# A recurrence and a routed mixture of experts on one core: layer two's matmuls after the last compaction, and five result buffers

## The chip, the core and the metric

The kernel runs on one core of a Trainium2 chip. A core has five engines that run side by side and meet only through semaphores: TensorE (PE) for matmuls and transposes, VectorE (DVE), ScalarE (ACT), GpSimd (POOL) and SyncE (SP). Matmuls write into PSUM, eight banks of 2 KB per partition; a bank holds 512 sums of 4 bytes for each of 128 partitions. DVE and ACT copy sums from PSUM to the on-chip memory SBUF; transfers between SBUF and the main memory are issued by SP, and, where rows are picked by an index, by POOL. The metric is the device time of one execution in microseconds (us); lower is better.

## The reference

```python
def _attn_ref(x, f_logit, lower_bound):            # x: 4 x 5056 x 256
    f = lower_bound + (1.0 - lower_bound) / (1.0 + np.exp(-f_logit))
    for t in range(S):
        h = f[:, t] * h + (1.0 - f[:, t]) * x[:, t]
        y[:, t] = h
...
def _moe_ref(x, w_gate, w1, w2):                   # N = 20224 rows, E = 8, F = 1024
    logits = x @ w_gate
    ...                                            # pairs by falling logit, at most N // E rows per expert
    for e in range(E):
        mask = assigned == e
        out[mask] = np.maximum(x[mask] @ w1[e], 0.0) @ w2[e]
```

A gated recurrence over 5056 time steps gives 20224 rows of 256 numbers. Every row is given to one of eight experts, 2528 rows to each, best logits first. An expert is two dense layers, 256 to 1024 with a relu and 1024 to 256.

## The kernel before

A first stage (to about 200 us) computes the recurrence with DVE scans, writes the rows to the buffer `hbuf` in main memory and collects the logits. The routing of the experts, one after the other, is a search on DVE with small matmuls. For each expert a *compaction* (`compact`, line 500) turns the mask of its rows into a list of row numbers; its matmuls write to the two PSUM banks `rt` and `rc` (lines 748 and 749). Routing and compaction of later experts run in small pieces (`tick`, line 1078) between the matmuls of the experts before them. The last compaction belongs to expert 7.

The rest is the experts' layers, in `moe` (line 755). An expert has 20 tiles of 128 rows, the last of 96, and they are worked in *chunks* of four tiles, five chunks per expert; expert 0 has six, and expert 7 six of 4, 4, 4, 4, 2 and 2 tiles. Layer one of a chunk is cut into eight blocks j of 128 hidden columns, and one block is a *step* of the loop at line 1098. A step holds, in PE's order:

- `first(k, c, j)`: six matmuls of 512 columns (the tiles' rows side by side) into a bank `pw`. There are six because every float32 number is split into a high and a low part (`xh`, `xl`, `w1h`, `w1l`) and three of the four products are kept, for each half of the 256 inputs. ACT then writes `hh`, the relu's high part, and DVE `hl`, its low part.
- in steps 3 and 5 (`TJ`), `trans`: the transposes `pt` of the next chunk's gathered rows `xg`, one half of the inputs in each.
- `second(...)`, layer two of the block three steps earlier (`LAG`): for each tile three matmuls of 256 columns, `hh` with the high part of w2, `hh` with its low part, `hl` with the high part, all added into the same 256 columns of a bank `py`, two tiles to a bank. So the last block of a chunk comes in step 2 of the next chunk; behind it ACT copies each bank to a result buffer `y` (pool `yp`, `YB` of them), which holds a pair of tiles.

POOL issues the transfers of this part: gathers of rows (`xg`, one per tile), stores of results (`out_dram`, one per tile), and three loads of weights per expert (`r`). They stand in one list, `issues`. `gather` appends a chunk's four (for the chunk after next, in step 0); `second` appends a chunk's stores; `load_w` puts its three at the list's front. At the end of each step one entry leaves the list (line 1125), and it waits on the chip for the newest `hh` that ACT had been given by then (`gate`). Three things take more than one out at once, and what stands ahead with it: `trans` forces the gathers that it is about to read (line 915), `split` the weights, and the claim of a result buffer all stores that are `YB` or more pairs old (line 977).

```python
            tc.add_manual_dep(st.ins, gate[-1].ins.name, SYNC, reason="one transfer per step")
...
            issue(upto=lambda what: what == ("g", k, c))
...
                issue(upto=lambda what: what[0] == "s" and what[1] <= turn - YB)
...
        issue(1 if i < len(todo) else 99, paced=i < len(todo))
```

The order on PE, DVE and ACT is the order in which this code emits instructions. A rough cost table (`Pace`) decides only when a waiting evacuation (`post`, `flush`) or a piece of the routing is emitted.

Of the kernel before, what the change touches and what calls it, by code (L numbers as in the profile page):

```python
# [7 lines left out]
F32 = mybir.dt.float32  # L8
# [5 lines left out]
AF = mybir.ActivationFunctionType  # L14
OP = mybir.AluOpType
# [91 lines left out]
def kernel(ctx: ExitStack, tc: tile.TileContext, x: bass.AP, f_logit: bass.AP,  # L107
# [643 lines left out]
    with tc.manual_schedule(engines={mybir.EngineType.PE, mybir.EngineType.DVE, mybir.EngineType.Activation}):  # L751
        moe(ctx, tc, locals())


def moe(ctx, tc, g):
    pace = g["pace"]
    nc = Paced(tc.nc, pace)
    v = nc.vector
    P, E, F, D, CAP, FB = (g[k] for k in ("P", "E", "F", "D", "CAP", "FB"))
    hbuf, w1, w2, out, ident_r, omlb, route, compact, rt, rc, ohp, ROW = (  # L760
        g[k] for k in ("hbuf", "w1", "w2", "out", "ident_r", "omlb", "route", "compact", "rt", "rc", "ohp", "ROW"))
# [3 lines left out]
    gp = ctx.enter_context(tc.tile_pool(name="gp", bufs=3))  # L765
    xp = ctx.enter_context(tc.tile_pool(name="xp", bufs=2))
    hp = ctx.enter_context(tc.tile_pool(name="hp", bufs=5))
    YB = 3
    yp = ctx.enter_context(tc.tile_pool(name="yp", bufs=YB))
    tps = ctx.enter_context(tc.tile_pool(name="tps", bufs=1, space=PSUM))  # L770
    pws = ctx.enter_context(tc.tile_pool(name="pws", bufs=3, space=PSUM))
    pys = ctx.enter_context(tc.tile_pool(name="pys", bufs=2, space=PSUM))
# [12 lines left out]
    WI, IDS, RAW, WS, XG, XS, HS, PY, SC = {}, {}, {}, {}, {}, {}, {}, {}, []  # L785
# [7 lines left out]
    issues = []  # L793
# [4 lines left out]
    def issue(n=1, upto=None, paced=False):  # L798
        st = None
        if upto is not None:  # L800
            n = max([x + 1 for x, (what, _) in enumerate(issues) if upto(what)], default=0)
        for _ in range(min(n, len(issues))):
            st = issues.pop(0)[1]()
            if paced and gate:

                tc.add_manual_dep(st.ins, gate[-1].ins.name, SYNC, reason="one transfer per step")
        return st
# [58 lines left out]
    def tiles(k, c):  # L866
        b, n = CHUNKS[k][c]
        return [min(P, CAP - (b + q) * P) for q in range(n)]

    def ids_at(k, c, q, n):  # L870
        b = CHUNKS[k][c][0] + q
        return off(IDS[k][:n, b:b + 1])
# [77 lines left out]
    def store(k, c, r, n, y):  # L950
        def emit():
            st = nc.gpsimd.indirect_dma_start(out=out, out_offset=ids_at(k, c, r, n), in_=y[:n, r % 2],
                                              in_offset=None)
            for o in SC:
                tc.declare_no_dep(st.ins, o.ins, reason="each row belongs to one expert")
            SC.append(st)
            return st
        return emit

    def second(k, c, j):  # L960
        hh, hl = HS.pop((k, c, j))
        w2s = WS[k][2]
        ns = tiles(k, c)
        for q, n in enumerate(ns):
            if j == 0 and q % 2 == 0:
                PY[q // 2] = pys.tile([P, 2, D], F32, name="py")
            if q:
                tick()
            py = PY[q // 2][:n, q % 2]
            a = slice(q * P, q * P + n)  # L970
            mm = [(hh[:, a], w2s[:, j, 0]), (hh[:, a], w2s[:, j, 1]), (hl[:, a], w2s[:, j, 0])]
            for i, (x, w) in enumerate(mm):
                nc.tensor.matmul(py, x, w, start=(j == 0 and i == 0 and q % 2 == 0),
                                 stop=(j == FB - 1 and i == 2), skip_group_check=True)
            if j == FB - 1 and q % 2 == 1:
                turn = len(SC) // 2 + sum(what[0] == "s" for what, _ in issues) // 2
                issue(upto=lambda what: what[0] == "s" and what[1] <= turn - YB)
                y = yp.tile([P, 2, D], F32, name="y")
                m = min(ns[q - 1:q + 1])
                if m == P:  # L980
                    nc.scalar.activation(y, PY[q // 2], AF.Copy)
                else:
                    nc.scalar.activation(y[:, 0], PY[q // 2][:, 0], AF.Copy)
                    nc.scalar.activation(y[:n, 1], py, AF.Copy)
                issues.extend((("s", turn), store(k, c, r, ns[r], y)) for r in (q - 1, q))

    class Bg:
        def __init__(self, gen, apart=0):
# [2 lines left out]
        def tick(self, force=False, within=None):  # L991
            if self.done:
                return False
            if within is not None:
                self.wait = min(self.wait, int(within))
            if not force:
                if self.wait:
                    self.wait -= 1
                    return False
                if not pace.due(self.need[0], self.need[1:], SLACK):  # L1000
                    return False
            try:
                self.need = next(self.gen)
                self.wait = self.apart
            except StopIteration:
                self.done = True
            return True
# [5 lines left out]
    comp, prog = {}, {}  # L1013
# [84 lines left out]
    for i in range(len(todo) + LAG):  # L1098
        step = i
        flush(i - 2 if i < len(todo) else i)  # L1100
        if i < len(todo):
            k, c, j = todo[i]
            if (c, j) == (0, 0) and k:
                assert wn == k + 1
                sp.until(lambda: sp.done)
                sp = None
            first(k, c, j)
            sp0.tick(True)
            tick()
            NS = len(CHUNKS[k])  # L1110
            if gathers:

                kk, cc = gathers[0]
                ahead = order.index((kk, cc)) - order.index((k, c))
                if ahead == 1 and j >= 1 or ahead == 2 and j >= (2 if (k, c) == (0, 0) else 0) and have(
                        kk, "ids", sum(CHUNKS[kk][cc])):
                    gather(*gathers.pop(0), soon=ahead == 1 or c == len(CHUNKS[k]) - 2 and j > 0)
            at = T0 if (k, c) == (0, 0) else TJ
            nxt = order.index((k, c)) + 1
            if j in at and nxt < len(order):  # L1120
                trans(*order[nxt], at.index(j))
        while made < first_lag.get(i, i - LAG + 1):
            second(*todo[made])
            made += 1
        issue(1 if i < len(todo) else 99, paced=i < len(todo))
        tick()
# [27 lines left out]
```

## Time and profile before

| | us |
|---|---|
| median of 3 runs | 1202.95 |
| the runs | 1202.89 to 1203.13 |
| the profiled execution, its own time | 1202.51 |
| its span | 1200.7 |
| PE busy | 1172.0 (98%) |
| DVE busy | 770.7 (64%) |
| ACT busy | 524.6 (44%) |
| POOL busy | 452.4 (38%) |

The span is what the profiler saw between the first and the last instruction; the execution's own time has 1.8 us around it. A share of busy time is a mean over stages with different limits, so the rows below are taken from stretches. In them a matmul's duration is longer than its distance from the next one, since matmuls are pipelined; what a matmul costs is read from the starts of a run of them.

### The profile page before, as it was taken

What the parts mean: (1) busy time and instruction counts of PE and PEld (TensorE: products, weight loads), DVE (VectorE), ACT (ScalarE), POOL (GpSimd) and SP (SyncE); (2) the same over time, 40 slices, a digit from 0 to 9 for tenths busy, and PEclk for the clock granted to TensorE, in tenths of its full rate; (3) what the DMA queues carried; (4) which work ended last, traced back from release to release, by engine and by line L of the source; (5) the groups of instructions that cost most, each with busy time, mean ns of one, the idle gap of its engine ahead of it and who ended that gap; (6) DMA issues with size and microseconds to landing.
All of it is one profiled execution on the core that took longest, in us unless ns stands there. A gap on an engine that the chain in (4) does not pass through costs nothing.

```text
span 1200.7 us, 23258 instructions
## 1 busy us (share of the span) xinstructions
PE 1172.0 (98%) x9152; PEld 1063.3 (89%) x9152; DVE 770.7 (64%) x1935; ACT 524.6 (44%) x1098; POOL 452.4 (38%) x458
## 2 busy tenths in 40 slices
PE   7999986999999999999999999999999999999997
PEld 7999965888988898888888888899889998999997
DVE  6999878878878977978788878423532243222222
ACT  7888813423533632632452345522642243223322
POOL 5777703332433324333333333333343334333322
PEclk9999998999999999999999999999999999999999
DMA  9999993112112212211211113111311131111111
GB/s 334 375 355 363 345 327 100 46 41 92 55 49 67 74 38 86 75 40 41 82 66 49 41 42 100 47 57 45 102 53 49 50 102 58 49 46 46 43 39 35
DMA packets 51869, 123.14 MB, mean 103 GB/s; under 512 B 7984, under 2 KB 28208, under 8 KB 50864
## 3 DMA queue, kind: packets, MB, share of 16 engines
q0 software_dynamic: 18960, 58.87, 15.7%
q1 hardware_dynamic: 32256, 62.78, 15.0%
q8 instruction: 72, 1.18, 0.4%
q14 instruction: 37, 0.30, 0.1%
q10 hardware_dynamic: 544, 0.01, 0.0%
HBM read 79.56 MB, written 42.07 MB: 101 GB/s over the span
## 4 chain that ended last, share of the span: by engine, by line
PE 61%; issue 19%; POOL 10%; DVE 4%; DMA 1%; POOLq 0%; ACT 0%; ACTq 0%; DVEq 0%; SPq 0%
PE py L100 25%; PE pw L100 24%; POOL out_dram L100 4%; POOL xg L100 4%; PE rt L100 4%; PE pr L100 4%; PE pb L100 2%; PE pf L100 2%; PE pt L100 1%; DVE MK L100 1%; POOL r L100 1%; DVE g L100 1%; DMA out_dram<-y,ids 0%; DMA fl<-in_f_logit_dram 0%; DMA xg<-hbuf,ids 0%
## 5 line engine op out<-in xcount | busy, mean ns | idle before, releaser
L100 PE MATMUL py<-w2s,hh 128*128 128x256 f32 (+1 forms) x2560 | 486.5, 287 | 0.6 <-ACT y L100 0.5
L100 ACT ACTIVATE hh<-pw 128x512 fp32r<-128x512 f32 (+3 forms) x336 | 192.5, 573 | 563.5 <-PE pw L100 541.2
L100 PEld LDWEIGHTS py<-w2s,hh 128*128 128x128 f32 (+1 forms) x2560 | 405.2, 187 | 19.2 <-ACT y L100 1.2
L100 DVE SCALAR_TENSOR_TENSOR hl<-pw,hh 128x512 fp32r<-128x512 f32 (+3 forms) x336 | 220.3, 656 | 313.7 <-ACT hh L100 312.6
L100 PE MATMUL py<-w2s,hl 128*128 128x256 f32 (+1 forms) x1280 | 361.3, 282 | 0.0
L100 POOL DMA_INDIRECT xg<-hbuf,ids x160 | 158.8, 992 | 313.9 <-ACT hh L100 292.6
L100 POOL DMA_INDIRECT out_dram<-y,ids x160 | 161.9, 1012 | 302.6 <-ACT hh L100 245.7
L100 PE MATMUL pw<-xh,w1h 128*128 128x512 f32 (+3 forms) x672 | 256.1, 383 | 2.4 <-DVE hl L100 1.7
L100 PE MATMUL pw<-xl,w1h 128*128 128x512 f32 (+3 forms) x672 | 257.7, 385 | 0.0
L100 PE MATMUL pw<-xh,w1l 128*128 128x512 f32 (+3 forms) x672 | 257.0, 384 | 0.0
L100 PEld LDWEIGHTS py<-w2s,hl 128*128 128x128 f32 (+1 forms) x1280 | 239.4, 187 | 0.0
L100 PEld LDWEIGHTS pw<-xh,w1l 128*128 128x128 f32 x672 | 125.9, 188 | 22.6
L100 PEld LDWEIGHTS pw<-xh,w1h 128*128 128x128 f32 x672 | 126.3, 189 | 14.4 <-DVE hl L100 1.9
L100 PEld LDWEIGHTS pw<-xl,w1h 128*128 128x128 f32 x672 | 126.0, 188 | 12.2 <-DVE r L100 0.2
L100 POOL TENSOR_TENSOR xl<-fl,xl 128x1024 f32<-128x1024 f32 (+1 forms) x39 | 92.3, 2366 | 42.8 <-ACT fl L100 35.1
L100 DVE TENSOR_TENSOR_SCAN g<-fg,g,pb 128x512 f32<-128x512 f32 (+4 forms) x78 | 92.8, 1227 | 9.9 <-ACT fg L100 8.9
L100 ACT ACTIVATE junk<-rt,r 128x158 bf16<-128x158 f32 x155 | 58.8, 392 | 53.9 <-DVE r L100 53.6
L100 PE MATMUL pr<-iw,g 128*128 128x136 f32 x632 | 79.8, 279 | 0.0
L100 PEld LDWEIGHTS pr<-iw,g 128*128 128x128 f32 x632 | 75.9, 190 | 0.1
L100 ACT ACTIVATE fg<-pf,one,nomlb 128x512 f32<-128x512 f32 (+1 forms) x80 | 57.4, 767 | 1.9
L100 ACT ACTIVATE y<-py 128x512 f32<-128x512 f32 (+2 forms) x88 | 48.1, 559 | 21.6 <-PE py L100 6.8
L100 DVE TENSOR_TENSOR xl<-pt,xh 128x512 fp32r<-128x512 f32 (+1 forms) x80 | 53.9, 674 | 0.6 <-ACT xh L100 0.3
(178 smaller groups left out, 1183.1 us busy)
## 6 DMA issues: line engine op xcount, KB each, us to landing
hbuf<-hr SPq DMA_DIRECT2D x39, 528.0 KB, 8.7
fl<-in_f_logit_dram SPq DMA_DIRECT2D x39, 512.0 KB, 5.9
xl<-in_x_dram SPq DMA_DIRECT2D x39, 512.0 KB, 6.1
xg<-hbuf,ids POOLq DMA_INDIRECT x160, 2.8
out_dram<-y,ids POOLq DMA_INDIRECT x160, 2.4
r<-in_moe_w_dram,wi POOLq DMA_INDIRECT x25, 4.5
hbuf<-hr SPq DMA_DIRECT2D x1, 264.0 KB, 9.1
fl<-in_f_logit_dram SPq DMA_DIRECT2D x1, 256.0 KB, 5.7
```

Of the source, the lines that this page charges most:

```text
L100: r = f(*args, **kw)
```

## The change

From the first chunk whose layer two begins after expert 7's compaction has ended, the two matmuls of a tile that share `hh` become one of 512 columns: the high and the low part of w2 lie side by side, and each gets its own 256 sums. A tile then fills a whole bank, the first two of a chunk in `py`, the third in `rt`, the fourth in `rc`. The matmul with `hl` adds to the first half. After a tile's last block ACT copies the second half to the result buffer, and DVE adds the first half to it. Apart from that, there are five result buffers in place of three, for the whole kernel.

```diff
-    YB = 3
+    YB = 5
...
+        if j == 0:
+            wides = len(ns) if E - 1 in comp and comp[E - 1].done else 0
+
+        def total(q):
+            y = Y[q // 2][:ns[q], q % 2]
+            v.tensor_tensor(y, PY[q][:ns[q], 0], y, op=OP.add)
+
+        def put(*qs):
+            issues.extend((("s", turn), store(k, c, r, ns[r], Y[r // 2])) for r in qs)
...
+                PY[q] = (pys.tile([P, 2, D], F32, name="py") if not wide or q < 2 else
+                         (rt, rc)[q - 2].tile([P, 512], F32, name="rt").rearrange("p (a d) -> p a d", a=2))
...
+            if wide:
+                nc.tensor.matmul(PY[q][:n], hh[:, a], w2s[:, j], start=(j == 0), stop=False, skip_group_check=True)
+                nc.tensor.matmul(PY[q][:n, 0], hl[:, a], w2s[:, j, 0], start=False, stop=last, skip_group_check=True)
...
+            if 0 < q <= wides:
+                total(q - 1)
+                if q % 2 == 0:
+                    put(q - 2, q - 1)
...
+            if wide:
+                nc.scalar.activation(Y[q // 2][:n, q % 2], PY[q][:n, 1], AF.Copy)
...
+            if wide and q == len(ns) - 1:
+                total(q)
+                put(q - 1, q)
```

Three places show what it does to the engines' orders. The first is PE in the first step with the merged form (third chunk of expert 5): `pt` are transposes, `py` and `rt` the banks of layer two.

```order
 L100 MATMUL pt<-identr,xg 128x128 x4
-L100 MATMUL py<-w2s,hh 128x256 x2
+L100 MATMUL py<-w2s,hh 128x512
 L100 MATMUL py<-w2s,hl 128x256
-L100 MATMUL py<-w2s,hh 128x256 x2
-L100 MATMUL py<-w2s,hl 128x256
-L100 MATMUL py<-w2s,hh 128x256 x2
-L100 MATMUL py<-w2s,hl 128x256
-L100 MATMUL py<-w2s,hh 128x256 x2
+L100 MATMUL py<-w2s,hh 128x512
 L100 MATMUL py<-w2s,hl 128x256
+L100 MATMUL rt<-w2s,hh 128x512
```

Each tile has two matmuls where it had three; the transposes keep their place ahead of layer two.

The second is ACT around the end of a late chunk, of before:

```order
L100 ACTIVATE xh<-pt 128x512
L100 ACTIVATE hh<-pw 128x512 x5
L100 ACTIVATE y<-py 128x512 x2
L100 ACTIVATE hh<-pw 128x512
L100 ACTIVATE xh<-pt 128x512
```

and now:

```order
L100 ACTIVATE xh<-pt 128x512
L100 ACTIVATE hh<-pw 128x512 x4
L100 ACTIVATE y<-py 128x256
L100 ACTIVATE hh<-pw 128x512
L100 ACTIVATE y<-py 128x256
L100 ACTIVATE y<-rt 128x256 x2
L100 ACTIVATE hh<-pw 128x512
```

The fifth `hh`, that of step 2, stood ahead of the copies and now stands behind the first of them. (On DVE the four additions stand between the `hl` of two steps.)

The third is POOL's list from the middle of expert 6's time on, before (`r` are weights, `xg` gathers, `out_dram` stores):

```order
L100 DMA xg<-hbuf,ids 128x264 x4
L100 DMA out_dram<-y,ids 20224x256 x2
L100 DMA r_12494<-in_moe_w_dram,wi 128x1024 x2
L100 DMA r_12495<-in_moe_w_dram,wi 128x2048
L100 DMA out_dram<-y,ids 20224x256 x2
L100 DMA xg<-hbuf,ids 128x264 x4
L100 DMA out_dram<-y,ids 20224x256 x5
L100 DMA xg<-hbuf,ids 128x264 x4
L100 DMA out_dram<-y,ids 20224x256 x5
```

and now, from a little earlier:

```order
L100 DMA xg<-hbuf,ids 128x264 x4
L100 DMA out_dram<-y,ids 20224x256 x4
L100 DMA xg<-hbuf,ids 128x264 x4
L100 DMA out_dram<-y,ids 20224x256 x4
L100 DMA xg<-hbuf,ids 128x264 x3
L100 DMA xg<-hbuf,ids 96x264
L100 DMA out_dram<-y,ids 20224x256 x4
L100 DMA xg<-hbuf,ids 128x264 x7
L100 DMA out_dram<-y,ids 20224x256 x4
L100 DMA xg<-hbuf,ids 128x264
L100 DMA r_12423<-in_moe_w_dram,wi 128x1024 x2
L100 DMA r_12424<-in_moe_w_dram,wi 128x2048
```

Stores no longer leave five in a row; they leave in fours, and seven gathers stand together once.

## Rows read from the trace of the kernel before

**Rows 1.** The profile's head and its line on PE: busy time, share of the span, instructions.

```profile
span 1200.7 us, 23258 instructions
PE 1172.0 (98%) x9152; PEld 1063.3 (89%) x9152; DVE 770.7 (64%) x1935; ACT 524.6 (44%) x1098; POOL 452.4 (38%) x458
```

**Rows 2.** Busy time by stretch, late in the layers: the stretch, its length, busy us of each engine with its instructions, then the granted clock, the DMA engines' share and GB/s.

```profile
800.00:900.00 100.00, 99.93 (x666) 90.53 (x665) 40.50 (x86) 44.63 (x102) 34.58 (x37) 1.00 0.20 64
900.00:1000.00 100.00, 99.79 (x656) 90.81 (x656) 35.90 (x53) 36.15 (x61) 35.57 (x37) 1.00 0.21 66
```

**Rows 3.** The chain that ended last, in order of time, in the middle of expert 7: start, length, what; `pw` are the six matmuls of a step's layer one (512 columns), `py` the twelve of its layer two (256 columns).

```profile
1095.07 1.40 PE pw L100 x6
1096.47 1.44 PE py L100 x12
...
1099.30 1.43 PE py L100 x12
1100.73 1.38 PE pw L100 x6
```

**Rows 4.** PE's instructions in order of time at the three places where ACT's copy waited for a store (start, length, what; in brackets the idle time ahead and what ended it), and the line of tile `y` on what ACT waited for (us, times).

```profile
626.67 0.27 PE L100 MATMUL py<-w2s,hl 128*128 128x256 f32 x1
627.22 0.38 PE L100 MATMUL py<-w2s,hh 128*128 128x256 f32 x1 [0.28 <-ACT y L100]
...
876.06 0.28 PE L100 MATMUL py<-w2s,hl 128*128 128x256 f32 x1
876.41 0.50 PE L100 MATMUL py<-w2s,hh 128*128 128x256 f32 x2
...
992.23 0.28 PE L100 MATMUL py<-w2s,hl 128*128 128x256 f32 x1
992.72 0.50 PE L100 MATMUL py<-w2s,hh 128*128 128x256 f32 x2 [0.21 <-ACT y L100]
...
  DMA out_dram<-y,ids: 6.2, 3
```

**Rows 5.** POOL's transfers in order of time: a chunk's end with stores in a burst, and the first and the fourth gather of a chunk four chunks later.

```profile
1014.74 0.97 POOL L100 DMA_INDIRECT out_dram<-y,ids  x1 [0.45 <-ACT y L100]
1016.01 0.97 POOL L100 DMA_INDIRECT out_dram<-y,ids  x1 [0.30 <-issue]
1017.28 0.97 POOL L100 DMA_INDIRECT out_dram<-y,ids  x1 [0.30 <-issue]
...
1105.85 0.99 POOL L100 DMA_INDIRECT xg<-hbuf,ids  x1 [1.92 <-ACT hh L100]
...
1114.68 0.94 POOL L100 DMA_INDIRECT xg<-hbuf,ids  x1 [1.89 <-ACT hh L100]
```

**Rows 6.** PE in order of time around steps 2 and 3 of that chunk: the last matmul of step 2's layer one, the last of the first tile's layer two, the transposes of step 3, and those of step 3 a chunk later.

```profile
1104.55 0.39 PE L100 MATMUL pw<-xh,w1l 128*128 128x512 f32 x1
...
1105.02 0.28 PE L100 MATMUL py<-w2s,hl 128*128 128x256 f32 x1
...
1107.61 0.46 PE L100 MATMUL pt<-identr,xg 128*128 128x128 f32 x4
...
1130.93 0.46 PE L100 MATMUL pt<-identr,xg 128*128 128x128 f32 x4
```

**Rows 7.** ACT at the same place: `hh` of step 2, `hh` of step 3 and the copy of the transposes behind it.

```profile
1104.98 0.60 ACT L100 ACTIVATE hh<-pw 128x512 fp32r<-128x512 f32 x1 [2.24 <-PE pw L100]
...
1107.81 0.60 ACT L100 ACTIVATE hh<-pw 128x512 fp32r<-128x512 f32 x1 [0.80 <-PE pw L100]
1108.31 0.59 ACT L100 ACTIVATE xh<-pt 128x512 fp32r<-128x512 f32 x1
```

**Rows 8.** A gather that PE waited for, early in the layers, in order of time; and of tile `xg` the time from a gather's start to its landing, and all that PE waited for it (us, times).

```profile
197.22 1.37 POOL L100 DMA_INDIRECT xg<-hbuf,ids  x1 [0.30 <-issue]
...
200.44 0.36 PE L100 MATMUL pt<-identr,xg 128*128 128x128 f32 x2 [0.93 <-DMA xg<-hbuf,ids]
...
  PE pt L100: 0.9, 1
...
DMA to landing us min/median/max: 2.7/2.8/3.8
```

**Rows 9.** Forms of ACT's and DVE's instructions behind 870 us: engine, operation, names, shapes, count, busy us, mean ns, idle time ahead.

```profile
L100 ACT ACTIVATE y<-py 128x256 f32<-128x256 f32 x3 | 1.1, 383 | 2.8 <-PE py L100 2.5
...
L100 DVE SCALAR_TENSOR_TENSOR hl<-pw,hh 128x256 fp32r<-128x256 f32 x8 | 3.4, 424 | 10.1 <-ACT hh L100 10.1
```

**Rows 10.** The end of the chain: start, length, what (a "q" is the engine's sequencer).

```profile
1191.71 2.87 PE py L100 x24
...
1194.61 0.38 ACT y L100
1194.99 0.28 ACTq L1150
1195.27 0.97 POOL out_dram L100
```

**Rows 11.** PE around 200 us by stretch (length, busy us, granted clock, DMA share, GB/s), and its longest idle time there, in order of time.

```profile
190.00:194.00 4.00, 1.10 (x7) 0.66 0.40 129
194.00:198.00 4.00, 4.00 (x33) 0.50 0.49 156
202.00:206.00 4.00, 2.31 (x17) 1.00 0.66 210
...
205.82 0.50 PE L100 MATMUL pw<-xh,w1h 128*128 128x256 f32 x2 [1.69 <-DVE hl L100]
```

More of the change, by code (lines that the diff above doesn't have):

```diff
@@ L958, in store @@
         return emit
+    Y, wides, turn = {}, 0, 0
     def second(k, c, j):
+        nonlocal wides, turn
         hh, hl = HS.pop((k, c, j))
@@ L963, in second @@
         ns = tiles(k, c)
+        last = j == FB - 1
+        if j == 0:
[5 more added lines that the diff above has]
+            issues.extend((("s", turn), store(k, c, r, ns[r], Y[r // 2])) for r in qs)
         for q, n in enumerate(ns):
-            if j == 0 and q % 2 == 0:
-                PY[q // 2] = pys.tile([P, 2, D], F32, name="py")
+            wide = q < wides
+            if j == 0 and (wide or q % 2 == 0):
+                PY[q] = (pys.tile([P, 2, D], F32, name="py") if not wide or q < 2 else
+                         (rt, rc)[q - 2].tile([P, 512], F32, name="rt").rearrange("p (a d) -> p a d", a=2))
@@ L967, in second @@
             if q:
                 tick()
-            py = PY[q // 2][:n, q % 2]
             a = slice(q * P, q * P + n)
[L971 to L975, printed above, removed]
+            if wide:
+                nc.tensor.matmul(PY[q][:n], hh[:, a], w2s[:, j], start=(j == 0), stop=False, skip_group_check=True)
+                nc.tensor.matmul(PY[q][:n, 0], hl[:, a], w2s[:, j, 0], start=False, stop=last, skip_group_check=True)
+            else:
+                py = PY[q - q % 2][:n, q % 2]
+                mm = [(hh[:, a], w2s[:, j, 0]), (hh[:, a], w2s[:, j, 1]), (hl[:, a], w2s[:, j, 0])]
+                for i, (x, w) in enumerate(mm):
+                    nc.tensor.matmul(py, x, w, start=(j == 0 and i == 0 and q % 2 == 0), stop=(last and i == 2),
+                                     skip_group_check=True)
@@ L976, in second @@
+            if not last:
+                continue
+            if 0 < q <= wides:
+                total(q - 1)
+                if q % 2 == 0:
+                    put(q - 2, q - 1)
+            if q % 2 == 0:
                 turn = len(SC) // 2 + sum(what[0] == "s" for what, _ in issues) // 2
                 issue(upto=lambda what: what[0] == "s" and what[1] <= turn - YB)
[L978 to L981, printed above, removed]
+                Y[q // 2] = yp.tile([P, 2, D], F32, name="y")
@@ L982, in second @@
+            if wide:
+                nc.scalar.activation(Y[q // 2][:n, q % 2], PY[q][:n, 1], AF.Copy)
+            elif q % 2 == 1:
+                y = Y[q // 2]
+                if n == P:
+                    nc.scalar.activation(y, PY[q - 1], AF.Copy)
                 else:
-                    nc.scalar.activation(y[:, 0], PY[q // 2][:, 0], AF.Copy)
+                    nc.scalar.activation(y[:, 0], PY[q - 1][:, 0], AF.Copy)
                     nc.scalar.activation(y[:n, 1], py, AF.Copy)
-                issues.extend((("s", turn), store(k, c, r, ns[r], y)) for r in (q - 1, q))
+                put(q - 1, q)
@@ L987, in moe @@
+            if wide and q == len(ns) - 1:
+                total(q)
+                put(q - 1, q)
     class Bg:
```

## The prediction

> **What bounds the kernel now.** I read the page first, for who is busy: the span is 1200.7 us and PE is busy in 98% of it [rows 1]. A busy PE is not yet a bound, so I took the table of stretches next: from 800 us on PE is busy in 99.8 to 99.9 of 100 us, while DVE, ACT and POOL stand at 35 to 45 [rows 2]. The chain of waits then says what a stretch of this part consists of: nothing but layer-one and layer-two matmuls in turn, a step of 6 and 12 of them [rows 3]. So here a nanosecond off a matmul is a nanosecond off the time, and so is every nanosecond for which PE has to wait; work on ACT, DVE and POOL costs nothing until it hands PE something late. The views to read next are therefore the few waits of PE that exist [rows 4], and how far ahead of PE the transfers run [rows 5 to 8].
>
> **Merged matmuls.** The program of after holds 416 matmuls of 512 columns in layer two, each in place of two of 256, from the third chunk of expert 5 on (13 chunks, 52 tiles, 8 blocks each). Twelve matmuls of 256 columns take 1.43 to 1.44 us, so 119.7 ns each; six of 512 columns in layer one take 1.38 to 1.40 us, so 231.7 ns each [rows 3]. A pair of 239.4 ns becomes one of 231.7: 7.7 ns, times 416 is 3.2 us less, all of it on the path. Bounds: 0, if a 512-column matmul of layer two runs like two of 256, and 3.9 us, if it takes 230 ns (the shortest six). I take 3.2, since the layer-one matmul has the same form and types. The Trainium skill (TensorE: Matmul & The Clock Gate, section Back-to-back issue gap) puts the gap at the columns over 2.4 GHz and 2.5 ns; by that a merge saves 2.5 ns and all of them 1.0 us. The rows show more per matmul than this, and I follow the rows.
>
> **Five result buffers: what they give.** In three places ACT could not copy layer two's sums out because the result buffer's store had not landed (6.2 us of ACT's time), and PE then waited for its bank [rows 4]. From start to start PE lost 0.55, 0.35 and 0.49 us less the usual 0.12: 0.43 + 0.23 + 0.37 = 1.0 us. With five buffers no copy waits so: 1.0 us less.
>
> **Five result buffers: what they cost.** This is the part that decides. The transfers leave one list, one per step. A chunk has 8 steps and puts 8 transfers on the list, 4 gathers (at its step 0, for the chunk after next) and 4 stores (at its step 2, of the chunk before). Each expert adds 3 loads of weights, which go to the front. So the list falls 3 steps further behind per expert, unless something forces more than one out. In before that is the claim of a result buffer: with three buffers a store may be at most two pairs late, and the surplus goes out in bursts at a chunk's end, as in the stores 1.27 us apart at 1014.74, 1016.01 and 1017.28 [rows 5]. Gathers then run far ahead: the one that starts at 1114.68 is read by the transposes at 1130.93, 16 us later [rows 5, 6]. With five buffers a store may be four pairs late, a whole chunk later. I followed the list of after through the code: from expert 3's third chunk on it is so long that the gathers of the next chunk leave in steps 7, 0, 1 and 2, and their first transposes stand in PE's queue behind layer one of step 3. No more delay is possible only because that place forces the rest out. The program's POOL order shows the same: strictly 4 stores, 4 gathers, and only once per expert a run of 7 gathers, which the claim of a buffer forces out. After such a run one or two chunks are in time; 18 of the last 24 chunks are not (9 before the merged form reaches the chunk's end, 9 after).
>
> What one late gather costs is read off before, where a transfer leaves in that very slot, the end of step 2. POOL starts it at 1105.85, released by ACT's hh that starts at 1104.98 [rows 5, 7]. A gather lands 2.8 us after its start (2.7 to 3.8) [rows 8], at 1108.65, and PE needs 0.04 more. The fourth transpose of step 3 starts about 0.22 after the row's 1107.61, at 1107.83 [rows 6]. So PE waits 0.86 us. That a late gather does stop PE, the profile shows once: a gather started at 197.22 held the transposes until 200.44 [rows 8].
>
> In the merged chunks it is worse. There ACT's order is no longer hh of step 2, then the results; the first tile's copy comes ahead of that hh. It must wait until the first tile's last matmul ends, about 1105.30 (the row at 1105.02 and 0.28) [rows 6], and takes 383 ns [rows 9], of which the next instruction overlaps 0.10 (1107.81 to 1108.31 for a 0.60 us instruction) [rows 7]. So hh starts at 1105.34 + 0.28 = 1105.62 in place of 1104.98, 0.64 later, and the gather that waits for it as well: 1.50 us per chunk.
>
> Sum: 9 x 0.86 + 9 x 1.50 = 7.7 + 13.5 = 21.2 us more. Bounds: 18 x 0.76 = 13.7 us, if gathers land after 2.7 and hh's delay costs nothing, and 9 x 1.01 + 9 x 1.65 = 23.9 us, if they land 0.15 later than the median, as some do. The Trainium skill (DMA: Bandwidth & Descriptors, section Anatomy of one DMA — SWDGE (gpsimd) path) fits a transfer at 2.0 us and its bytes over 436 GB/s; for a gather of 135 KB that is an estimate of 2.3 us, and by it 18 waits would be 0.5 us shorter each and the time 1211. The profile has 2.8 for this very transfer, and it decides.
>
> **Copies, sums and banks.** A tile now costs ACT 383 ns for the lower half and DVE an addition, nearest to the 424 ns of a 256-column DVE instruction that reads PSUM too [rows 9]. Over 52 tiles that is 20 us on ACT, in place of 26 copies of some 0.6, and 22 us on DVE in some 300 us, on engines that are busy 36 to 45 in 100 there [rows 2]. A bank is next written one layer one and three tiles later, 1.39 + 3 x 0.351 = 2.4 us; copy, addition and one hh between them need 0.38 + 0.42 + 0.60 = 1.4. That cover is thin only in the last two chunks of two tiles (six and three matmuls of 256 columns, 0.72 + 0.35 = 1.07 us): some 0.2 us once. DVE's hl behind the additions is read three steps later, so nobody waits for it. At the end, before has the first store 0.69 us behind the last matmul (copy 0.38, hand-over 0.28) [rows 10]; after, the first tile's copy starts 0.32 before that end, its addition ends near 0.5 and the store starts near 0.8: 0.1 us more. Together 0.3 us, bounds 0 and 1.
>
> **Total.** 21.2 - 3.2 - 1.0 + 0.3 = 17.3 us more. The profiled execution took 1202.51 us, so 1219.8; the median of the runs is 0.44 above it, so 1220.2.
>
> **Rivals.** (1) *The gathers stay ahead*, because the list is shorter than I followed it to be; then only the gains count: 1202.95 - 3.2 - 1.0 + 0.1 = 1198.9. For it: in before no transpose after 201 us waits for a gather [rows 8]. Against it: the order of the rows on POOL's queue, which no timing changes. It decides as soon as the fourth gather leaves a step earlier, since a step (2.8 us) is more than the whole wait. (2) *Only the slot counts*: hh's delay is absorbed, and all 18 waits are 0.86: 15.5 - 3.9 = 11.6 more, 1214.5. (3) *The merge saves nothing*: 1223.4. (4) *The clock falls after each wait.* Around 190 us, where PE was busy for little of several us, the granted clock was 0.66 and 0.50 in two stretches of 4 us, a loss of 3.4 us [rows 11]; 18 of these would give 1220 + 61 = 1281. Against it: an idle stretch of 1.69 us before 205.82 left the clock at 1.00 [rows 11], and here PE is dense for 20 us between waits. The Trainium skill (TensorE: Matmul & The Clock Gate, section A second HAM failure mode: psum-queue depth-cycling) does describe such a fall for 512-column matmuls that cycle through banks with small gaps; the row with 1.69 us speaks against it here.
>
> **Chances.** Forecast 0.70, with its own range 1215 to 1225; (2) 0.14, (3) 0.03, (4) 0.03, (1) 0.08, and 0.02 that a few late gathers just use up the gains. The range 1212 to 1226 holds the first three. About 0.2% (2.4 us) is what a measurement of this kernel can tell from no change: slower by more 0.90, within 0.02, faster 0.08.
>
> **What would show it.** Right: PE waits on gathers at pt about 18 times, some 20 us in all, with 0.8 to 0.9 us each until about 900 us and 1.5 after; the fourth gather of a chunk starting about 1 us ahead of its transposes; no wait of ACT for a store; a merged tile in 351 ns in place of 359. Wrong: no waits at pt (then rival 1), waits of one size (2), a granted clock under 0.99 behind 600 us (4), or new waits at py for a DVE addition, which I hold to be 0.2 us.

## The result and the profile after

The changed kernel takes 1218.64 us (median of 4 runs, 1218.22 to 1219.17); the kernel before, run beside it, 1202.92 (1202.0 to 1203.13). The ratio is 1.0133, 95% interval 1.012 to 1.0145: slower by 15.7 us, where the prediction had 17.3 and a range of 9 to 23. The profiled execution took 1218.7 us with a span of 1216.9, so the spans differ by 16.2 us.

The head of the page, and its line on PE, against [rows 1]:

```profile
span 1216.9 us, 22509 instructions
PE 1170.3 (96%) x8736; PEld 1041.6 (86%) x8736; DVE 791.2 (65%) x1987; ACT 525.6 (43%) x1121; POOL 452.7 (37%) x458
```

PE has 416 matmuls fewer (9152 in [rows 1]), as the change says. Its share fell from 98 to 96%, so the lost time is idle time of PE. The table of stretches (length; busy us and instructions of PE, PE's weight loads, DVE, ACT, POOL; granted clock, DMA share, GB/s) says where, beside [rows 2]:

```profile
800.00:900.00 100.00, 98.08 (x651) 88.73 (x650) 40.38 (x85) 42.73 (x98) 34.95 (x37) 1.00 0.21 65
900.00:1000.00 100.00, 96.15 (x507) 81.36 (x505) 38.50 (x63) 35.75 (x66) 35.12 (x37) 1.00 0.21 66
1000.00:1100.00 100.00, 93.88 (x491) 79.40 (x492) 35.69 (x61) 29.23 (x59) 31.97 (x33) 1.00 0.14 45
```

PE loses 2 us in 100 where layer two still has its old form, and 4 to 6 with the merged form; the granted clock stays at 1.00. The first row of PE's waits (us, times, the longest) names one cause:

```profile
PE pt L100 <- DMA xg<-hbuf,ids: 18.9, 19, 2.0
```

One of the 19 is the early wait that before had too [rows 8]; 18 are new. The view of tile `xg` adds what POOL waited for ahead of its gathers, and how long gathers take to land:

```profile
  ACT y L100: 20.9, 9
...
DMA to landing us min/median/max: 2.6/2.8/3.9
```

For nine gathers the wait is put down to a copy `y` on ACT, which no gather reads. What it is, one such place shows, of all engines in order of time (start, length; in brackets the idle time ahead), to be laid beside [rows 6, 7]:

```profile
996.06 0.39 PE L100 MATMUL pw<-xh,w1l 128*128 128x512 f32 x1
...
996.52 0.28 PE L100 MATMUL py<-w2s,hl 128*128 128x256 f32 x1
...
996.84 0.38 ACT L100 ACTIVATE y<-py 128x256 f32<-128x256 f32 x1 [2.00 <-PE py L100]
...
997.12 0.59 ACT L100 ACTIVATE hh<-pw 128x512 fp32r<-128x512 f32 x1
...
997.98 0.95 POOL L100 DMA_INDIRECT xg<-hbuf,ids  x1 [2.44 <-ACT y L100]
...
999.06 0.37 PE L100 MATMUL pt<-identr,xg 128*128 128x128 f32 x3
1000.87 0.28 PE L100 MATMUL pt<-identr,xg 128*128 128x128 f32 x1 [1.44 <-DMA xg<-hbuf,ids]
```

Read it from the top. Layer one of step 2 ends at 996.45, and `hh` could start then. But the copy stands ahead of it on ACT and waits for the first tile's last matmul (996.52 and 0.28). So `hh` starts at 997.12, 0.63 us late. It ends at 997.71, and POOL, which waits for it, starts the fourth gather at 997.98, 1.08 us ahead of the transposes that read it, where 2.8 are needed. Three transposes run; the fourth, due some 0.2 behind the first, at 999.25, comes at 1000.87: 1.6 us lost. The view's idle time of 1.44 is shorter, since it counts the third transpose as busy to its end.

The same place in a chunk of the old form:

```profile
804.30 0.60 ACT L100 ACTIVATE hh<-pw 128x512 fp32r<-128x512 f32 x1 [2.23 <-PE pw L100]
...
805.16 0.92 POOL L100 DMA_INDIRECT xg<-hbuf,ids  x1 [1.89 <-ACT hh L100]
...
806.92 0.37 PE L100 MATMUL pt<-identr,xg 128*128 128x128 f32 x3
807.85 0.27 PE L100 MATMUL pt<-identr,xg 96*128 96x96 f32 x1 [0.55 <-DMA xg<-hbuf,ids]
```

Here `hh` comes at once, the gather starts 1.76 us ahead of the transposes, and PE loses 0.7. Measured so, from the start of the transpose ahead, the 9 waits of the old form are 0.33 to 0.97 us and 6.8 in sum, the 9 of the merged form 1.33 to 2.23 us and 14.2 in sum: 21.0 us.

The chain of waits, away from such a place, has what the merge gives, against [rows 3]:

```profile
1099.90 1.40 PE pw L100 x6
1101.30 0.70 PE py L100 x4
1101.99 0.70 PE rt L100 x4
1102.70 1.39 PE pw L100 x6
```

Layer two of a step, now 4 matmuls into `py` and 4 into `rt`, takes 1.40 us where 12 took 1.43 to 1.44. At 0.04 a step, 104 full steps (52 tiles of eight blocks, four tiles to a step) give 4.2 us; by the rounding of these rows 3 to 5. And the end, against [rows 10]:

```profile
1210.37 0.73 ACT L100 ACTIVATE y<-py 128x256 f32<-128x256 f32 x2 [2.05 <-PE py L100]
1210.40 0.28 PE L100 MATMUL py<-w2s,hl 128*96 128x256 f32 x1
1210.78 0.77 DVE L100 TENSOR_TENSOR y<-py,y 128x256 f32<-128x256 f32 x2 [2.04 <-ACT y L100]
1211.48 0.97 POOL L100 DMA_INDIRECT out_dram<-y,ids  x1 [6.54 <-DVE y L100]
```

The first store leaves 0.80 us behind the last matmul (1210.68), 0.11 later than before. No copy of after waits for a store. So 21.0 for the gathers, less 1.0 for those waits, less about 4 for the merge, and 0.1 at the end make 16.1, where the spans differ by 16.2.

### The profile page after: what moved, and what is told of

It reads as the page before. It is cut to its first block, busy times and chain, and to the rows that moved or that the text cites. A ratio compares the mean times of both kernels' runs of the same rounds, so it can differ in the third digit from the quotient of the medians.

```text
span 1216.9 us, 22509 instructions
## 1 busy us (share of the span) xinstructions
PE 1170.3 (96%) x8736; PEld 1041.6 (86%) x8736; DVE 791.2 (65%) x1987; ACT 525.6 (43%) x1121; POOL 452.7 (37%) x458
## 4 chain that ended last, share of the span: by engine, by line
PE 61%; issue 18%; POOL 9%; DVE 4%; DMA 3%; ACT 1%; POOLq 0%; DVEq 0%; SPq 0%
PE pw L100 24%; PE py L100 20%; PE rt L100 8%; POOL xg L100 4%; POOL out_dram L100 4%; PE pr L100 3%; DMA xg<-hbuf,ids 3%; PE pb L100 2%; PE pf L100 1%; PE pt L100 1%; DVE MK L100 1%; DVE g L100 1%; POOL r L100 1%; ACT y L100 1%; DMA fl<-in_f_logit_dram 0%
## 5 line engine op out<-in xcount | busy, mean ns | idle before, releaser
L100 PE MATMUL py<-w2s,hh 128*128 128x256 f32 (+2 forms) x1952 | 416.0, 301 | 0.0
L100 PEld LDWEIGHTS py<-w2s,hh 128*128 128x128 f32 (+1 forms) x1952 | 315.7, 188 | 20.4 <-DVE y L100 0.2
L100 PE MATMUL py<-w2s,hl 128*128 128x256 f32 x1088 | 306.7, 282 | 0.0
L100 PEld LDWEIGHTS py<-w2s,hl 128*128 128x128 f32 x1088 | 204.0, 187 | 2.7
L100 PE MATMUL rt<-w2s,hh 128*128 128x512 f32 x192 | 71.4, 394 | 0.0
L100 PEld LDWEIGHTS pt<-identr,xg 128*128 128x128 f32 (+1 forms) x320 | 35.9, 140 | 29.7 <-DMA xg<-hbuf,ids 21.6
```

Source lines behind the costliest of these rows:

```text
L100: r = f(*args, **kw)
```

## The experiments

The theory: five buffers remove the claims that kept the list of transfers short; the fourth gather of a chunk then leaves in step 2, and PE waits for it in step 3; in the merged form the copy ahead of `hh` makes it later still. Rivals: the merge or its extra instructions cost the time; the five buffers cost by something other than the list; the lateness is a fixed one that a later use would hide. The first four below ran on one chip (before: 1204.44 us), the other four on another (before: 1202.83), so the ratios are compared. Each edit is made to after unless the text says otherwise.

**Three buffers with the merged form.**

```diff
-    YB = 5
+    YB = 3
```

> The merged matmuls with three result buffers as before. Theory A (the list of transfers runs late because five buffers let the stores wait, so gathers reach PE late): no wait of PE for a gather behind 300 us; what is left is the merge, 3.2 to 3.9 us less than before, and the copies' waits for a store, about 1 us as before: 1199.5 us (1198.5 to 1200.5). Rival B (the merged form itself, its banks rt and rc and the copies that stand ahead of hh, costs the time): 1216 to 1219 us, as after the change.

Measured: 1202.28 us, ratio 0.9983 (0.9974 to 0.9992). The new waits are gone and with them the loss; the merge alone does no harm. The gain is smaller than expected, 2.2 us. ACT's row of waits for stores (us, times, the longest), and what PE loses by one, in order of time:

```profile
ACT y L100 <- DMA out_dram<-y,ids: 27.0, 12, 2.6
```

```profile
994.04 0.66 ACT L100 ACTIVATE y<-rt 128x256 f32<-128x256 f32 x2 [2.53 <-DMA out_dram<-y,ids]
...
994.94 0.50 PE L100 MATMUL rt<-w2s,hh 128*128 128x512 f32 x1 [1.12 <-DVE y L100]
```

Before has 3 such waits and 6.2 us of them [rows 4]. In the merged form a buffer is claimed with the first tile of a pair (here the third of its chunk), earlier than before, and its store has landed less often by then; PE loses 2.1 us in three places, not 1.0; 1.3 of them are at the place shown, and the other two places lie ahead of the merged form. Another 0.9 us lies in two pauses of PE at 475 to 477 us for which the profile shows no cause.

**Five buffers with the old form** (the edit is made to before).

```diff
-    YB = 3
+    YB = 5
```

> The kernel before with five result buffers and nothing else. Theory A: 18 waits of PE for a gather, each 0.75 to 0.86 us to the end, since no copy stands ahead of hh; 1.0 us less for the copies' waits: 1202.9 + 14.5 - 1.0 = 1216.4 us (1214 to 1218). Rival B: 1202 us, the copies' waits gone and nothing lost.

Measured: 1222.22 us, ratio 1.0147 (1.0131 to 1.0162). One number in the code makes the whole loss, without a merged matmul. It was more than expected. PE's waits:

```profile
PE pt L100 <- DMA xg<-hbuf,ids: 14.8, 18, 2.0
```

Of the 17 late ones 14 cost 0.6 to 0.9 us and one 1.1, as expected; but two, 124 us apart, cost 2.1 and 2.2. The first of these in order of time:

```profile
829.62 0.38 PE L100 MATMUL pw<-xh,w1l 128*128 128x480 f32 x1
...
831.34 0.57 ACT L100 ACTIVATE hh<-pw 128x480 fp32r<-128x480 f32 x1 [3.47 <-PE py L100]
...
832.18 0.95 POOL L100 DMA_INDIRECT xg<-hbuf,ids  x1 [2.24 <-ACT hh L100]
...
834.92 0.28 PE L100 MATMUL pt<-identr,xg 128*128 128x128 f32 x1 [1.96 <-DMA xg<-hbuf,ids]
```

`hh` could start at 830.0, when layer one of its step ends, and starts 1.3 us later; the gather follows it. The rule (the gather leaves with that `hh`) holds; why ACT came late in these two chunks, both behind a run of six gathers, stays open. In sum PE waits 16.8 us; less 1.0 for the copies that is 15.8, at the lower end of the interval (15.8 to 19.5). The clock adds to it, as PE by stretch shows (length, busy us, granted clock, DMA share, GB/s):

```profile
832.00:836.00 4.00, 2.04 (x16) 1.00 0.22 67
836.00:840.00 4.00, 4.00 (x18) 0.57 0.00 0
840.00:844.00 4.00, 4.00 (x32) 1.00 0.09 33
956.00:960.00 4.00, 1.97 (x14) 1.00 0.22 67
960.00:964.00 4.00, 4.00 (x29) 1.00 0.00 0
```

Behind the first of the two long waits, in which PE was idle for 1.96 us, the granted clock fell to 0.50, the lower of its two levels (1.2 GHz), for some 3.3 us; behind the second, with 2.03 us, it stayed at 1.00. From the late transpose to the start of the second layer one after it are 5.88 us in the first place (834.92 to 840.80) and 4.36 in the second (959.28 to 963.64): 1.5 us lost. With them the account is 17.3 us of the 17.8 measured.

**Two transfers a step while the list is long.**

```diff
-        issue(1 if i < len(todo) else 99, paced=i < len(todo))
+        issue((2 if len(issues) > 8 else 1) if i < len(todo) else 99, paced=i < len(todo))
```

> The changed kernel with one line more: a step sends two transfers while more than eight stand in the list. Theory A: the waits for gathers (18, 21.0 us from start to start) are gone, and so are those for a store: 1218.6 - 21 = 1197.8 us (1197 to 1199). Rival B: no change, 1217 to 1219 us. Rival C (two more buffers slow the memory or the copies): no change either, 1217 to 1219 us.

Measured: 1199.3 us, ratio 0.9953 (0.994 to 0.9967), 5.1 less, as expected. All five buffers and all merged matmuls are still there; only the list is kept short, and no late gather is waited for. So neither the buffers nor the merged form cost the time by themselves. ACT's copies wait again, as their row shows, and a stretch of PE late in the layers is full all the same:

```profile
ACT y L100 <- DMA out_dram<-y,ids: 20.1, 8, 2.6
```

```profile
900.00:1000.00 100.00, 100.00 (x531) 84.93 (x529) 42.44 (x69) 36.85 (x69) 36.75 (x38) 1.00 0.21 68
```

**The same in before with five buffers.**

```diff
-    YB = 3
+    YB = 5
...
-        issue(1 if i < len(todo) else 99, paced=i < len(todo))
+        issue((2 if len(issues) > 8 else 1) if i < len(todo) else 99, paced=i < len(todo))
```

> The kernel before with five result buffers and two transfers per step while more than eight stand in the list; no merged matmuls. It prices the copies' waits for a store by themselves. Theory A: 1202.9 - 1.0 = 1201.9 us (1201.4 to 1202.4), no wait of ACT for a store. Rival C: 1214 us or more, as with five buffers alone.

Measured: 1202.44 us, ratio 0.9983 (0.9974 to 0.9992): 2.0 less (1.0 to 3.1); 1.0 was expected. No copy waits for a store. Beside the run above, which differs by the merged form alone and ran on the same chip, the merge is worth 1202.44 - 1199.3 = 3.1 us.

**Transposes one step later.**

```diff
-    TJ, T0 = (3, 5), (5, 6)
+    TJ, T0 = (4, 6), (5, 6)
```

> The changed kernel with the next chunk's transposes in steps 4 and 6 in place of 3 and 5, so one step later. Theory A: the list falls behind until the place that forces it out stops it, wherever that is; the fourth gather then leaves at the end of step 3 and PE waits again, some 22 times for 0.8 to 0.95 us (the copy that delays hh of step 2 no longer stands ahead of that gather): 1217 us (1215 to 1219). Rival D (the gathers are late by a fixed amount of at most 1.6 us, for which a step of 2.8 us is enough): no waits, 1198 us.

Measured: 1225.64 us, ratio 1.0202 (1.0184 to 1.0219), above the 1215 to 1219 expected. A step more between gather and use would hide a fixed lateness. It hides nothing: the list lets go of the fourth gather a step later too, because only the transposes force it out.

```profile
PE pt L100 <- DMA xg<-hbuf,ids: 21.7, 24, 2.3
```

The rival of a fixed lateness falls. This kernel is slower than after by 7.0 us, in the spans of the profiled executions by 6.2. The late gathers, 23 in place of 18, cost 24.2 us, 3.2 more than in after; three of them, some 123 us apart and each right behind an expert's three loads of weights, cost 1.8 to 2.5 us each. The rest is the clock (the same columns as in the table of five buffers with the old form):

```profile
206.00:210.00 4.00, 4.00 (x25) 0.61 0.25 68
...
984.00:988.00 4.00, 2.31 (x12) 1.00 0.80 284
988.00:992.00 4.00, 3.91 (x15) 0.57 0.09 33
992.00:996.00 4.00, 4.00 (x24) 1.00 0.09 33
```

It fell to 0.50 behind two idle stretches of PE, one of 1.77 us before 205.65 us and one of 1.78 us before 988.09, the last of those three gathers. The matmuls behind the first took 4.32 us where the same ones took 2.94 in after, and those behind the second 6.20 where the same ones took 4.54 a little later (from 995.68): 1.4 and 1.7 us lost. With the 3.2 of the waits that makes 6.3 us, where the spans differ by 6.2. Behind the other two of the three gathers, with 1.68 and 2.29 us of idle time, the clock stayed at 1.00. Among the four runs the longest, 1229.94 us, has the lowest mean granted clock, 0.990; the others have 0.993 to 0.995.

**Gathers at the front of the list.**

```diff
-                    gather(*gathers.pop(0), soon=ahead == 1 or c == len(CHUNKS[k]) - 2 and j > 0)
+                    gather(*gathers.pop(0), soon=True)
```

> The changed kernel with every chunk's gathers put ahead of all stores in the list. Theory A: no wait of PE for a gather, and five buffers give the stores time enough: 1197.8 us (1197 to 1200). Rival B: 1217 to 1219 us.

Measured: 1197.52 us, ratio 0.9958 (0.9943 to 0.9973), span 1195.2. Gathers now stand ahead, and it is the stores that wait in the list; the only wait of PE for a gather that is left is the early one. PE by stretch:

```profile
900.00:1000.00 100.00, 100.00 (x528) 84.87 (x527) 41.84 (x68) 36.35 (x68) 40.56 (x41) 1.00 0.22 71
1000.00:1100.00 100.00, 100.00 (x526) 84.81 (x525) 34.32 (x59) 28.98 (x59) 34.05 (x35) 1.00 0.15 47
```

**`hh` ahead of the first copy.**

```diff
             if wide:
+                if q == 0:
+                    flush(step)
                 nc.scalar.activation(Y[q // 2][:n, q % 2], PY[q][:n, 1], AF.Copy)
```

> The changed kernel with hh of step 2 given to ACT ahead of the first tile's copy; the list as after the change. Theory A: still 18 waits, but those of the merged chunks fall from about 1.5 to 0.9 us, 9 x 0.64 = 5.8 us less: 1212.8 us (1211.5 to 1214). Rival B (the copies cost by other means than the gather's release): under 2 us less, 1217 us.

Measured: 1212.83 us, ratio 1.0083 (1.0067 to 1.0098): 5.8 to 6.0 us less than after, as 9 x 0.64 has it. The waits, and one place of the merged form:

```profile
PE pt L100 <- DMA xg<-hbuf,ids: 12.9, 19, 1.2
```

```profile
1019.37 0.60 ACT L100 ACTIVATE hh<-pw 128x512 fp32r<-128x512 f32 x1 [2.17 <-PE pw L100]
1019.86 0.66 ACT L100 ACTIVATE y<-py 128x256 f32<-128x256 f32 x2
...
1020.23 0.95 POOL L100 DMA_INDIRECT xg<-hbuf,ids  x1 [1.82 <-ACT y L100]
...
1021.94 0.38 PE L100 MATMUL pt<-identr,xg 128*128 128x128 f32 x3
1023.09 0.28 PE L100 MATMUL pt<-identr,xg 128*128 128x128 f32 x1 [0.77 <-DMA xg<-hbuf,ids]
```

There are as many waits as in after, but those of the merged form are now 0.7 to 1.0 us (one 1.4), the size of the old form's: the difference of the two groups was the place of one ACT instruction. (The view names `y` as what POOL waited for; it is `hh`, which ends at 1019.97; the start at 1020.23 is 0.26 behind it, as 805.16 is behind the `hh` that ends at 804.90.)

**Both: catch up, and `hh` first.**

> The changed kernel with both: two transfers per step while more than eight stand in the list, and hh of step 2 ahead of the first copy. Theory A: no waits are left that hh's delay could lengthen, so this is the catch-up alone but for the last bank, 0.2 us less: 1197.6 us (1196.8 to 1198.8).

The two edits above in one kernel. Measured: 1197.46 us, ratio 0.9956 (0.9943 to 0.997). It and the one with gathers at the front are the fastest of the study, 0.4% below the kernel before, and not told apart from each other.

## Why the prediction came true, step by step

- *PE is the bound, and every wait of it is time.* Right: 21.0 us of waits, less the gains, are the span's 16.2.
- *The list falls behind, and 18 gathers are late, 9 and 9.* Right, in number and place. That three buffers had kept the list short by their claims is shown from three sides: the buffers alone make the loss, a list that is kept short takes it away with five buffers in place, and so does a list that holds stores back in place of gathers.
- *0.86 us each in the old form, 7.7 in sum.* The mechanism held, the size was 0.75 and 6.8: the gather at 805.16 landed after 2.65 us, at the short end of 2.6 to 2.8, and three waits were under 0.7.
- *0.64 more in the merged form, 13.5 in sum.* 14.2. `hh` was 0.63 late where it was read, and its place was worth the expected 6 us when it was put back. Eight of the nine waits make 12.0, as 8 x 1.50 has it; the ninth is 2.23, since its gather (at 1144.29) landed after 3.5 us, which a forecast from the median leaves out. That the sum of both forms, 21.0, lies so near the 21.2 forecast is in part luck: 0.9 too much in the old form and 0.7 too little here nearly cancel. The Trainium skill (DMA: Bandwidth & Descriptors, section Anatomy of one DMA — SWDGE (gpsimd) path) would have a gather land after an estimated 2.3 us; the trace of after has 2.8 as its median, like that of before, and the measurement decides.
- *The merge saves 3.2 us.* Between the 3.1 of the pair of runs and the 4.2 of the chain. The Trainium skill (TensorE: Matmul & The Clock Gate, section Back-to-back issue gap) gave an estimated 1.0, from a formula that it states for an isolated matmul; these rows speak for three to four times that, and the measurement decides. The 416 matmuls lie in 14 chunks, the last two of two tiles, and not in 13; the sum goes by the 416.
- *No copy waits for a store, 1.0 less.* Right in after. The step was right for this kernel only: three buffers with the merged form lose more by it (2.1 us), and the catching up brings ACT's waits back without a loss of PE.
- *0.3 us for copies, additions, banks and the end.* About 0.1 at the end; a wait of 0.2 us of PE's weight load for DVE's addition comes once, as forecast for the last chunks.
- *The rivals.* Gathers stay ahead: refuted in after, and it is what the experiments without late gathers show, at 1197.5 to 1199.3 beside the 1198.9 worked out. Only the slot counts: refuted by the two sizes of wait, and with `hh` first it is what happens (1212.8 beside 1214.5). The merge saves nothing: refuted. The clock falls after each wait: refuted in after, where the granted clock is 1.00 in each stretch shown, and also from 1148 to 1152 us, behind the longest wait (2.05 us idle). But a single wait can bring it down. Of the five longest in the experiments (five buffers with the old form, transposes one step later), two did, at 1.5 and 1.7 us each, half of the 3.4 that the rival reckoned with. And the idle stretch before 205.82 us that spoke against this rival is weak evidence: at the same place one of 1.77 us did bring the clock down. The length does not tell which will, since 2.29 us did not; what does stays open.

## What to carry to other kernels

A buffer's claim can be what drives a queue: before adding buffers, ask which transfers the claim has been pushing out, and where the list would then let go of the rest. When a list that is paced one per step receives more than one per step on average, its length is set by whatever forces entries out; order it by when each is needed, or let it catch up. An instruction put ahead of another on an engine that works in program order delays all that hang on the second one, here a transfer on another engine and then the bound.

## What was not expected

- With three buffers the merged form makes ACT wait 27.0 us for stores, in place of 6.2, since the claim comes half a pair earlier; PE loses 2.1 us by it.
- With the catching up ACT waits 20.1 us for stores and PE nothing that can be seen: the same wait on ACT costs by where it lies, not by its length.
- The granted clock fell to 0.50 behind three idle stretches of PE of 1.77 to 1.96 us, in two of the experiments, and cost 1.4 to 1.7 us each on top of the wait; it did not fall behind others as long, and in after behind none of the 18.
- In two chunks of the old form with five buffers an `hh` starts 1.3 us behind its sums, with no reason in the view; the runs leave it open.
